# A scheduler that counts one-column matmuls by what they stream, with a new set of seeds

## The chip, the cores and the metric

The kernel runs on one core of one Trainium2 chip. The core has a matrix engine (TensorE, PE in the profile, with PEld for its weight loads), a vector engine (VectorE, DVE), a scalar engine (ScalarE, ACT) that evaluates functions such as exp, a general engine (GpSimd, POOL) and a queue that issues DMAs (SyncE, SP). Each engine works through its own queue in order and waits on semaphores where it needs another engine's result. The metric is the time of one execution on the device, in microseconds (us), as the median of the runs shown.

## What is computed

One transformer block with adaptive layer norm. The input x is 2048 rows of 512; there are 32 heads of 16 columns.

```python
mod = (silu(c) @ w_mod).reshape(1, 6, 1, 512)
sa, ca, ga, sb, cb, gb = (mod[:, i] for i in range(6))
h = layernorm(x) * (1 + ca) + sa
x = x + ga * mha(h, wqkv, wo)                  # 32 heads, softmax over 2048 keys
h = layernorm(x) * (1 + cb) + sb
x = x + gb * (gelu(h @ w1 + b1) @ w2 + b2)     # w1: 512 x 1376
```

All inputs are bfloat16. c is one row of 512, so each of the six modulation vectors is a product of one row with a 512 x 512 matrix. sa and ca are called the first modulation here (modA), sb and cb the second (modB).

## The kernel before

**Tiling.** Queries are worked in four blocks of 512 rows, keys in 16 tiles of 128. A run is one query block with four heads; there are 32 runs (in the last block each run has eight heads with half the queries). For each run and key tile PE makes four score blocks of 512 columns (L803), each with 128 keys as weights in 32 rows of the array (the columns of two heads, with the queries masked to one of them). A score block goes one of two ways:

- to ACT: the blocks are taken three and two at a time in turn (PSUM tiles st), and one instruction at L852 writes the exponentials (pt);
- to DVE: four blocks of a key tile go to PSUM tiles ax, and DVE turns them into the bit patterns of powers of two (L900, then shifted copies at L953 and L932 that are summed). POOL takes slices of 128 of the last shifted copy (L938) where it can work beside DVE.

The PV matmuls at L994 add all of these into one PSUM bank, od: per key tile four matmuls of 32 columns each, side by side in the array. At the end of a run DVE copies od out (L1019); the first PV matmul of the next run waits for that copy, since there is one od bank. The copy is divided by the row sums by way of DMAs and POOL (`normalise`, L1046), and the projection, second layer norm, Gelu (L1236) and MLP of each block are worked in between later runs (`block_tail`); those of the last half block come at the end (`last_half`).

**The order of the work.** It is not written by hand. A planner (`Plan`) runs while the program is built: it keeps, for each engine, the operations that are ready with a guessed duration, and repeatedly commits the one that can start first. Among operations that could start within a small slack of each other, `pick` takes the lowest of priority plus `spread`. `spread` is a pseudo-random number drawn from the operation's number and a seed; there is one seed for every 12.5 us of planned time (`SEEDS`), and a seed divisible by 4 gives no random part. So a seed changes the order of all that follows it.

**Zero matmuls.** `commit` keeps a list, `done`, of PE's operations of the last 30 us with the time that each is counted to have streamed. It walks back through the list until the sum reaches 1.45 us (`HEAT`); that operation's time plus 3.4 us (`WIN`) becomes `cool`. When the planner's time has passed `cool`, a PV operation gets a set of four zero matmuls with it (`extra`, L446 in `zeros`), and `step` may put in a matmul of zeros of its own (`heat`, L430, L435, or `zeros` at L446). Before the first scores `step` doesn't look at `cool` and fills every gap. `fill_at` is found in the same way with 1.6 us, and holds back work that isn't due.

**The modulations.** `mod_columns` makes eight columns for each modulation. A column is four matmuls whose moving operand is one column (L575), with 128 x 128 weights from w_mod. In the second modulation every other column is followed by a matmul of zeros with 384 columns (L578, `warmer`). The planner's duration for a column was 0.36 us in the second modulation and 0.22 us in the first, and these were also what `done` counted as streamed. A chain of such pieces is made by `chain`.

At the start the first modulation's weights (blk at L502) are loaded behind the first rows of x. DVE takes statistics of x (L599, L600), POOL makes 1/sqrt (L604, L606), DVE normalises (z, L610), PE transposes z (L652), and DVE and ACT apply the modulation (blk, L618 and L615). Then come keys and queries (L693), values (L732), the copy of the keys (kT, L623 on ACT), the masked queries (qm, L711), and the first scores.

Of the kernel before, what the change touches and what calls it, by code (L numbers as in the profile page):

```python
# [53 lines left out]
AL = 0.31  # L54
FILL = 1.6
SPREAD = 0.3
SEEDS = (0, 754, 829, 213, 501, 185, 582, 565, 437, 42, 790, 462, 0, 754, 457, 839, 409, 0, 203, 962, 735, 761, 634, 310, 991, 550, 943, 962, 775, 874, 0, 773, 813, 994, 107, 0, 718, 755, 523, 613, 695, 751, 275, 363, 273, 389, 697, 823, 85, 41, 155, 101, 0, 0, 0, 559, 994, 0, 0, 0, 0, 0, 0, 0, 0, 0)
HEAT = 1.45


class Res:


    def __init__(self, name, n, alloc):
        self.name, self.alloc = name, alloc
        self.free = [0.0] * n


class Op:
    count = 0  # L70

    def __init__(self, eng, fn, us, deps=(), lat=0.14, prio=5.0, mode=None, kind="", acq=None,
                 rel=(), gate=None, port=False):
        self.port = port
        self.eng, self.fn, self.us, self.lat, self.prio = eng, fn, us, lat, prio
        self.mode, self.kind, self.acq, self.rel, self.gate = mode, kind, acq, rel, gate
        self.end = None
        self.ready = 0.0
        self.tile = None
        self.slot = None  # L80
        self.kb, self.due, self.extra = 0, 1e9, False
        self.uses = 0
        self.rows, self.cont, self.run = None, False, None
        self.waiters = []
        self.todo = 0
        self.seq = Op.count
        Op.count += 1
        for d in deps:
            if d is None:
                continue  # L90
            if d.end is None:
                d.waiters.append(self)
                self.todo += 1
            else:
                self.ready = max(self.ready, d.end)
        for owner in rel:
            owner.uses += 1


class Plan:  # L100
# [51 lines left out]
    def spread(self, o):  # L152
        seed = SEEDS[min(int(self.now // 12.5), len(SEEDS) - 1)]
        x = (o.seq * 2654435761 ^ seed * 2246822519) & 0xFFFFFFFF
# [25 lines left out]
    def commit(self, s, o):  # L180
        self.lists[o.eng].remove(o)
        self.now = s
        if o.acq is not None:
            o.slot = min(range(len(o.acq.free)), key=lambda i: o.acq.free[i])
            o.acq.free[o.slot] = 1e18
            o.tile = o.acq.alloc(o.slot)
        if o.kind == "pv" and s >= self.cool and o.last_left() > 1:
            o.extra, o.us = True, 2 * o.us
        if o.rows is not None:
            o.row = min(o.rows, key=lambda i: self.tiles.get(i, 0.0) if self.mode == "qk" else i)  # L190
            o.mode = ("qk", o.row)
        if o.eng == "PE":
            self.done.append((s, (o.us if o.mode[0] != "qk" else o.us * (len(o.mode) - 1) / 4)))
            while self.done[0][0] < s - 30.0:
                self.done.popleft()
            tot = 0.0
            self.fill_at = self.cool = 0.0
            for t, us in reversed(self.done):
                tot += us
                if tot >= HEAT and not self.cool:  # L200
                    self.cool = t + WIN
                if tot >= self.fill:
                    self.fill_at = t + WIN
                    break
            if o.mode[0] != self.mode:
                self.mode, self.tiles = o.mode[0], {}
            for i in o.mode[1:]:
                self.tiles[i] = s + o.us
            self.free["PE"] = s + 0.01
        else:  # L210
            self.free[o.eng] = s + o.us
            if o.port:
                self.port[o.eng] = s + o.us
            if o.eng == "DVE" and o.us > 0:
                self.dve = (s, s + o.us, o.port)
        o.end = s + o.us + o.lat
        if o.kb:
            q = "SP"
            self.bus[q] = max(self.bus[q], s + o.us + 0.9) + o.kb / (300.0 if s < 12.0 else 260.0)
            o.end = self.bus[q] + 0.7  # L220
        if o.fn is not None:
            o.fn(o)
        for owner in o.rel:
            owner.uses -= 1
            owner.last = max(getattr(owner, "last", 0.0), o.end + (DVE_PE if o.eng == "DVE" else 0.0))
            if owner.uses == 0:
                owner.acq.free[owner.slot] = owner.last
        for w in o.waiters:
            w.todo -= 1
            w.ready = max(w.ready, o.end + (DVE_PE if o.eng == "DVE" and w.eng == "PE" else 0.0))  # L230
            if w.todo == 0:
                self.lists[w.eng].append(w)
# [21 lines left out]
def kernel(  # L254
# [57 lines left out]
    ps = scores.enter_context(tc.tile_pool(name="ps", bufs=1, space=psum))  # L312
# [81 lines left out]
    def chain(pieces, deps, kind, acq, rel=(), steps=1, need=None):  # L394

        first = prev = None
        at, step = due_now
        for n, (fn, us) in enumerate(pieces):
            last = n == len(pieces) - 1

            def go(o, fn=fn):
                if first is not None and o is not first:
                    o.tile, o.acq, o.slot = first.tile, first.acq, first.slot
                fn(o.tile)
            o = Op("PE", go, us, (tuple(deps) if prev is None else (prev,)) + (() if need is None else (need(n),)), lat=PEL if last else 0.0, mode=("full", 0),
                   kind=kind, acq=acq if prev is None else None, rel=rel if last else ())
            o.due = at + step * (steps * n // len(pieces))
            o.cont = prev is not None
            plan.add(o)
            first = first or o  # L410
            prev = o
        due_now[0] += steps * step
        return prev
# [165 lines left out]
                             rhs=warm[:, 0:1].to_broadcast([P, QB - P]))  # L579

    def mod_columns(dst, ws, kind, warmer=True):
        mm = chain([(lambda ps, n=n, w=w, m=m: mod_mm(ps, n, w[1](), m, warmer), 0.36 if warmer else 0.22)
                    for n, w in enumerate(ws) for m in range(NC)],
                   [o_sc, o_warm, ws[0][0]], kind, r_ax, [w[2] for w in ws],
                   need=lambda i: ws[i // NC][0])

        def out_(o):
            nc.vector.tensor_copy(out=dst, in_=mm.tile[:, 0:2 * NC])
            nc.vector.tensor_scalar(out=dst[:, NC:2 * NC], in0=dst[:, NC:2 * NC], scalar1=1.0,
                                    scalar2=None, op0=ALU.add)  # L590
        return op("DVE", out_, 0.4, (mm,), prio=0.65, rel=(mm,))
# [895 lines left out]
```

## Time and profile before

| | us |
|---|---|
| median of 3 runs (lowest, highest) | 780.99 (780.62, 781.88) |
| profiled execution, time | 779.58 |
| its span, first to last instruction | 777.8 |
| ACT busy | 750.5 |
| PE busy | 722.0 |
| DVE busy | 712.7 |
| POOL busy | 281.2 |

The profile is of one execution. Each line of a group gives the source line, the engine, the operation, what it writes and reads by the program's names, the count, then busy time and mean duration, then the idle time of the engine ahead of these instructions and what ended it. A line of a timeline gives the start, the duration and the instruction, and in brackets the idle time before it with its releaser. A line of the busy time by stretches gives the stretch, its length, then the busy time of PE, PEld, DVE, ACT and POOL with the number of instructions in brackets, the granted TensorE clock as a share of full speed, the DMA engines' share and GB/s. A line of the chain gives the start, the duration and the work that the end depended on.

### The profile page before, as it was taken

The page shows a single profiled execution, that of the slowest core. Times are in us where ns is not written, and L with a number is a line of the kernel's source. Part 1 is how long each engine was busy: PE and PEld are TensorE (multiplying, and loading weights), DVE is VectorE, ACT ScalarE, POOL GpSimd, SP SyncE. Part 2 cuts the span into 40 slices and gives each one's busy share as a digit, 9 for nine tenths or more (in the row PEclk, how much of TensorE's full clock was granted, in tenths as well). Part 3 has the DMA queues.
Part 4 walks back from the last instruction along what each step waited for, and adds up shares of the span by engine and source line. Part 5 has one row for each costly group of instructions (what it writes and reads, how often), then busy time and mean ns, then how long its engine had stood idle before and what let it go on. Part 6 is the DMA issues. An engine that isn't in the chain of part 4 may idle for free.

```text
span 777.8 us, 20624 instructions
## 1 busy us (share of the span) xinstructions
PE 722.0 (93%) x8233; PEld 274.2 (35%) x8307; DVE 712.7 (92%) x1180; ACT 750.5 (96%) x680; POOL 281.2 (36%) x622
## 2 busy tenths in 40 slices
PE   8888999999999889999998999999999999989998
PEld 3433333233333232323332323223234444434455
DVE  6777999999899999999999989999989998999964
ACT  3999999999999999999999999999999999999994
POOL 5221433444533334454444433333322423233320
PEclk9999998999999999999999999999999999999999
DMA  7033011000011010000100010000111000100010
GB/s 217 28 107 124 16 27 43 12 24 13 22 43 54 23 47 23 19 6 22 44 20 21 15 35 16 26 23 16 39 48 29 22 22 16 46 25 18 25 46 28
DMA packets 39074, 28.23 MB, mean 36 GB/s; under 512 B 17957, under 2 KB 34374, under 8 KB 38978
## 3 DMA queue, kind: packets, MB, share of 16 engines
q1 hardware_dynamic: 38970, 26.91, 12.1%
q8 instruction: 65, 1.06, 0.6%
q14 instruction: 31, 0.25, 0.1%
q10 hardware_dynamic: 8, 0.00, 0.0%
HBM read 21.30 MB, written 2.61 MB: 31 GB/s over the span
## 4 chain that ended last, share of the span: by engine, by line
ACT 50%; PE 27%; DVE 12%; issue 9%; DMA 1%; POOL 0%; SPq 0%; ACTq 0%; DVEq 0%; POOLq 0%
ACT pt L852 46%; PE od L994 9%; PE st L803 8%; DVE ph L900 5%; PE ax L1157 3%; DVE sh L953 2%; ACT g L1236 2%; PE ax L803 2%; DVE ph L953 1%; PE ax L693 1%; DMA blk<-in_w_mod_dram 1%; DVE sl L932 1%; DVE g L1227 1%; PE ax L1217 1%; PE t L1157 1%
## 5 line engine op out<-in xcount | busy, mean ns | idle before, releaser
L852 ACT ACTIVATE pt<-st 128x1536 bf16<-128x1536 f32 x626 | 708.6, 1408 | 4.4 <-PE st L803 2.3
L900 DVE TENSOR_SCALAR ph<-ax 128x512 int16<-128x512 f32 x484 | 318.1, 682 | 25.2 <-PE ax L803 22.3
L938 POOL TENSOR_TENSOR sl<-ph,step 128x128 int32<-128x128 int32 x358 | 163.7, 459 | 327.3 <-DVE sh L953 105.3
L803 PE MATMUL st<-qm,kT 32*128 32x512 bf16 x1564 | 245.7, 384 | 32.5 <-ACT pt L852 25.0
L803 PEld LDWEIGHTS <-kT 32*128 32x128 bf16 x2048 | 86.6, 91 | 244.1 <-issue 232.5
L803 PE MATMUL ax<-qm,kT 32*128 32x512 bf16 x484 | 162.5, 381 | 3.5 <-DVE ph L900 2.8
L994 PEld LDWEIGHTS <-VEB 128*32 128x32 bf16 x4992 | 109.6, 96 | 150.2 <-issue 128.0
L994 PE MATMUL od<-pt,VEB 128*32 128x512 bf16 (+1 forms) x1952 | 150.8, 344 | 0.9 <-ACT pt L852 0.5
L953 DVE TENSOR_SCALAR sh<-ph 128x4096 int16<-128x4096 int16 x121 | 146.9, 1217 | 2.5 <-PE od L994 2.2
L994 PE MATMUL od<-ph,VEB 128*32 128x512 bf16 (+1 forms) x1216 | 90.1, 340 | 1.7 <-DVE OD L1019 1.0
L994 PE MATMUL od<-sh,VEB 128*32 128x512 bf16 (+1 forms) x1216 | 84.6, 340 | 1.6 <-DVE sh L953 0.8
L953 DVE TENSOR_SCALAR ph<-ph 128x2048 int16<-128x2048 int16 x121 | 83.0, 687 | 0.4
L932 DVE TENSOR_SCALAR sl<-ph 128x1024 int16<-128x1024 int16 (+3 forms) x121 | 57.7, 482 | 0.4 <-PE od L994 0.4
L1046 POOL TENSOR_TENSOR OT<-OD,RB 128x128 bf16<-128x128 f32 x76 | 35.4, 470 | 48.1 <-DVE sh L953 14.8
L994 PE MATMUL od<-sl,VEB 128*32 128x512 bf16 (+1 forms) x608 | 48.4, 342 | 0.3
L1217 PE MATMUL ax<-blk,W 128*128 128x512 bf16 (+1 forms) x142 | 39.2, 358 | 2.0 <-issue 0.8
L1046 POOL TENSOR_TENSOR OS<-OD,RB 128x128 bf16<-128x128 f32 x48 | 22.8, 476 | 39.4 <-DVE sl L932 15.6
L693 PE MATMUL ax<-blk,w 128*128 128x512 bf16 x100 | 33.4, 383 | 3.3 <-ACT blk L615 1.7
L1227 DVE TENSOR_SCALAR g<-ax,b1c 128x512 bf16<-128x512 f32 (+1 forms) x41 | 28.0, 691 | 3.9 <-PE ax L1217 3.0
L1157 PE MATMUL ax<-w,g 128*128 128x512 bf16 x101 | 28.9, 381 | 1.1 <-DVE ph L900 0.6
L599 DVE BATCH_NORM_STATS2 ln_s<-xb 128x6 f32<-128x512 bf16 x32 | 21.6, 676 | 1.4 <-DMA xb<-in_A_x_dram 1.3
L1157 PEld LDWEIGHTS <-g 128*128 128x128 bf16 x176 | 13.7, 97 | 22.5 <-issue 12.8
(112 smaller groups left out, 400.8 us busy)
## 6 DMA issues: line engine op xcount, KB each, us to landing
RB<-rn SPq DMA_DIRECT2D x124, 64.0 KB
xb<-in_A_x_dram SPq DMA_DIRECT2D x8, 512.0 KB
out_dram<-o SPq DMA_DIRECT2D x16, 128.0 KB
qm<-qs SPq DMA_DIRECT2D x120, 16.0 KB
W<-in_B_w_dram SPq DMA_DIRECT2D x1, 1376.0 KB
w<-in_A_wqkv_dram SPq DMA_DIRECT2D x3, 384.0 KB
blk<-in_w_mod_dram SPq DMA_DIRECT2D x2, 512.0 KB
g<-in_w_mod_dram SPq DMA_DIRECT2D x2, 512.0 KB
```

Source lines behind the costliest of these rows:

```text
L693: return chain([(lambda ps, j=j: nc.tensor.matmul(out=ps[:, 0:QB], lhsT=w.tile[:, j, cc * P:(cc + 1) * P], rhs=o_h[b].tile[:, j, :], start ...
L803: nc.tensor.matmul(out=o.tile[:, k * QB:(k + 1) * QB], lhsT=kT[cc][kb][rows, ko * P:(ko + 1) * P], rhs=qm.tile[rows, par, :] if hb is None ...
L852: nc.scalar.activation(out=e.tile[:, 0:len(got) * QB], in_=o.tile[:, 0:len(got) * QB], func=ACT.Exp, scale=ESC)
L900: nc.vector.tensor_scalar(out=ph.tile[:, c0:c0 + QB], in0=o.tile, scalar1=PH_B, scalar2=0.0, op0=ALU.add, op1=ALU.max)
L932: parts = [in_turn(op("DVE", lambda o: nc.vector.tensor_scalar(out=into.tile[:, 0:cols], in0=first.tile[:, 0:cols], scalar1=PH_SH[-1], sca ...
L938: after_dve(nc.gpsimd.tensor_tensor(out=into.tile[:, c].bitcast(I32), in0=first.tile[:, c].bitcast(I32), in1=step, op=ALU.add))
L953: o = op("DVE", lambda o: nc.vector.tensor_scalar(out=dst(o), in0=src(), scalar1=PH_SH[j], scalar2=None, op0=ALU.add), us, deps, lat=DL, p ...
L994: nc.tensor.matmul(out=o_od[r].tile[32 * i:32 * i + 32, n * HB:n * HB + w], lhsT=v_tile(kt)[:, c0:c0 + 32], rhs=got[i][:, at:at + w], star ...
L1046: two = beside(lambda c: nc.gpsimd.tensor_tensor(out=OT.tile[:, c], in0=OD.tile[:, c], in1=o5.tile[:, c], op=ALU.mult), (OT,), (OD, o5))
L1157: nc.tensor.matmul(out=ps, lhsT=g[:, f, col:col + P], rhs=rhs, start=(f == 0), stop=(f == NF - 1))
L1217: mm = chain([(lambda ps, f=f, j=j: nc.tensor.matmul(out=ps[:, 0:N], lhsT=W1[:, j, f * P:(f + 1) * P], rhs=h.tile[:, j, 0:N], start=(j == ...
L1227: ev.append(op("DVE", lambda o, f=f, mm=mm: nc.vector.tensor_scalar(out=g.tile[:, f, 0:N], in0=mm.tile[:, 0:N], scalar1=b1c[:, f:f + 1], s ...
```

## The change

A third element is allowed in a piece of a chain: the time that the planner counts as streamed. Only `mod_columns` gives it, 0.18 us for a column with odd number and 0.01 for one with even number, in both modulations, though the first has no matmul of zeros behind its columns. The planned durations stay. Of the 66 seeds, eight near the end are zero in both kernels and all others differ; none of the first 49 is zero now, where five of them were before. Lines below 409 of the source move down by one.

```diff
-SEEDS = (0, 754, 829, 213, 501, 185, 582, 565, 437, 42, 790, 462, 0, 754, 457, 839, 409, 0, 203, 962, 735, 761, 634, 310, 991, 550, 943, 962, 775, 874, 0, 773, 813, 994, 107, 0, 718, 755, 523, 613, 695, 751, 275, 363, 273, 389, 697, 823, 85, 41, 155, 101, 0, 0, 0, 559, 994, 0, 0, 0, 0, 0, 0, 0, 0, 0)
+SEEDS = (589, 42, 869, 201, 842, 714, 286, 774, 871, 883, 670, 306, 195, 922, 117, 659, 193, 45, 151, 549, 170, 271, 319, 470, 749, 145, 287, 829, 529, 198, 510, 578, 819, 255, 730, 695, 454, 90, 99, 606, 462, 783, 435, 482, 134, 154, 446, 417, 301, 0, 693, 890, 0, 263, 0, 207, 778, 430, 526, 0, 731, 0, 0, 0, 0, 0)
...
-        self.kb, self.due, self.extra = 0, 1e9, False
+        self.kb, self.due, self.extra, self.act = 0, 1e9, False, None
...
-            self.done.append((s, (o.us if o.mode[0] != "qk" else o.us * (len(o.mode) - 1) / 4)))
+            self.done.append((s, o.act if o.act is not None else (o.us if o.mode[0] != "qk" else o.us * (len(o.mode) - 1) / 4)))
...
-        for n, (fn, us) in enumerate(pieces):
+        for n, (fn, us, *act) in enumerate(pieces):
...
             o.cont = prev is not None
+            o.act = act[0] if act else None
             plan.add(o)
...
-        mm = chain([(lambda ps, n=n, w=w, m=m: mod_mm(ps, n, w[1](), m, warmer), 0.36 if warmer else 0.22)
+        mm = chain([(lambda ps, n=n, w=w, m=m: mod_mm(ps, n, w[1](), m, warmer), 0.36 if warmer else 0.22, 0.17 * (m % 2) + 0.01)
                     for n, w in enumerate(ws) for m in range(NC)],
```

## The prediction

> **What bounds the kernel now.** First the busy shares and the costliest groups on the page.
>
> ```profile
> PE 722.0 (93%) x8233; PEld 274.2 (35%) x8307; DVE 712.7 (92%) x1180; ACT 750.5 (96%) x680; POOL 281.2 (36%) x622
> ...
> L852 ACT ACTIVATE pt<-st 128x1536 bf16<-128x1536 f32 x626 | 708.6, 1408 | 4.4 <-PE st L803 2.3
> ```
>
> ScalarE (ACT) is busy for 96% of the span, and 708.6 of its 750.5 us are the exponentials of L852: 1564 score blocks of 512 columns at 708.6/1564 = 0.453 us each. Between the first exponential (15.79) and the last (754) ACT does little but these, so the time is the start, plus ACT's work, plus ACT's gaps, plus the tail. The same group with its shapes kept apart:
>
> ```profile
> L852 ACT ACTIVATE pt<-st 128x1536 bf16<-128x1536 f32 x313 | 507.6, 1622 | 2.9 <-PE st L803 2.0 <-PE ax L803 0.9
> L852 ACT ACTIVATE pt<-st 128x1024 bf16<-128x1024 f32 x312 | 373.0, 1196 | 1.5 <-PE ax L803 1.0 <-PE st L803 0.3
> ```
>
> The records overlap: a pair lasts 1.622 + 1.196 = 2.82 us, yet five blocks advance by 5 x 0.453 = 2.27. So each record hides some 0.28 us, and a gap that is shown costs 0.28 more than its idle time. From start to start, the trace has 1.331 and 0.904 us where ACT is dense; what exceeds this I call a stall.
>
> Then busy time by stretches of 2 us around the largest gap, and ACT's own timeline there:
>
> ```profile
> 130.00:132.00 2.00, 1.73 (x24) 0.95 (x24) 2.00 (x4) 2.00 (x4) 0.30 (x1) 1.00 0.14 36
> 132.00:134.00 2.00, 1.68 (x15) 0.40 (x14) 2.00 (x3) 2.00 (x3) 0.46 (x1) 0.51 0.30 99
> 134.00:136.00 2.00, 2.00 (x19) 0.60 (x15) 1.09 (x6) 1.55 (x3) 0.43 (x1) 0.50 0.01 4
> 136.00:138.00 2.00, 2.00 (x20) 0.57 (x19) 1.43 (x6) 2.00 (x3) 1.27 (x3) 0.50 0.00 0
> 138.00:140.00 2.00, 2.00 (x27) 0.43 (x19) 1.66 (x4) 1.13 (x2) 0.46 (x1) 0.79 0.04 8
> ```
>
> ```profile
> 134.98 3.28 ACT L852 ACTIVATE pt<-st 128x1024 bf16<-128x1024 f32 x3 [0.45 <-PE ax L803]
> 139.13 11.40 ACT L852 ACTIVATE pt<-st 128x1536 bf16<-128x1536 f32 x10 [0.87 <-PE ax L803]
> ```
>
> The column ahead of the DMA share is the granted TensorE clock. It is halved for about 6.8 us from 132.0, and only here between start and tail. The 32 one-column matmuls of the second modulation (L575) run from 128.5 to 135.6: the clock falls in the middle of them. In the halved stretch PE is full and ACT waits twice.
>
> Third, the start, because the order changes there:
>
> ```profile
> 8.32 0.99 DVE L610 TENSOR_SCALAR z<-xb,mv,rs 128x512 bf16<-128x512 bf16 x2 [0.61 <-POOL rs L606]
> ...
> 10.37 0.71 DVE L589 TENSOR_SCALAR modA<-modA 128x4 f32<-128x4 f32 x1
> ...
> 11.19 0.99 DVE L618 TENSOR_SCALAR blk<-st,modA 128x512 bf16<-128x512 bf16 x2
> ...
> 11.77 1.45 ACT L615 ACTIVATE blk<-st,modA 128x512 bf16<-128x512 bf16 x2 [3.86 <-DVE blk L618]
> ...
> 15.79 6.88 ACT L852 ACTIVATE pt<-st 128x1536 bf16<-128x1536 f32 x6 [1.52 <-PE st L803]
> ...
> 25.12 0.59 ACT L623 CAST kT<-ax 128x512 bf16<-128x512 f32 x1 [1.11 <-PE ax L693]
> ...
> 26.20 3.71 ACT L852 ACTIVATE pt<-st 128x1536 bf16<-128x1536 f32 x3 [0.48 <-PE st L803]
> ```
>
> The normalised rows z are ready at 9.3, before the modulation's weights have landed (9.57), so they cost nothing. ACT later waits 1.11 and 0.48 us for the second block's keys.
>
> Last, the chain at one of the 31 changes from one run of heads to the next:
>
> ```profile
> 617.41 0.61 DVE OD L1019
> 618.02 0.04 issue
> 618.07 0.40 PE od L985 x4
> 618.47 0.87 PE od L994 x32
> 619.34 0.34 PE st L803 x2
> ```
>
> The single od bank must be copied out (L1019) before PE can go on, and od matmuls stand ahead of the next scores; ACT ran dry at 619.7 for 0.44 us, start to start.
>
> **The change, part by part.** *Work.* Counted by line and shape in the two orders of instructions, ACT, SP and all arithmetic of PE are the same in number. PE has 11 more full-width zero matmuls (26 to 32 at L430, 10 to 15 at L435) and one set of four fewer at L446 (104 to 100). POOL takes 15 more slices (358 to 373), and DVE's sl instructions shrink by 15 x 256 columns; by the sl forms (480, 546 and 611 ns for 1280, 1536 and 1792 columns) that is 15 x 0.066 = 1.0 us. DVE is idle 8% and ACT never waits on POOL, so I take 0; the ends are -1.0 and +0.5.
>
> *The second modulation.* Before, 24 one-column matmuls stand between score blocks 238 and 248, with one set of four PV matmuls among them. After, the 32 are spread over blocks 295 to 315, at most eight between two groups of scores, with two to five sets of PV matmuls in most gaps and one set of zeros at block 310. Streams of 512 columns follow each other 0.22 us apart (sixteen od matmuls in fours take 1.05, four alone 0.39). Over eight blocks (3.6 us) the leanest stretch streams 1.1 us before and 1.45 after. I take the dip as gone. It is worth 0.45 + 0.87 + 2 x 0.28 = 1.88 us. Ends: 0 (dip back) and -1.9.
>
> *The start.* Two things are put in order differently. DVE now has the modA copy and scale ahead of the four z; before they were behind. And PE has nine zero matmuls behind the modulation and ahead of the transposes. Step by step: modulation on PE ends at 10.1 as before (its DMAs are issued first, as before). modA is done by 10.6 (0.18, modB's price for the same scale) to 11.1 (0.71, its own row). The four z take 1.5 to 1.8 (rows 0.83 + 0.99, or 0.70 + 0.73 for the next block), to 12.1 to 12.9. The zeros end at 10.1 + 9 x 0.22 = 12.1, within that. Transposes then need 0.6 more, so DVE's blk starts about 13.2 to 13.5, not 11.19: +2.0 to +2.3. The q matmuls of the first three slices are now queued ahead of the last k matmul, which gains about 0.4. The first exponential comes at 17.4 to 17.7: +1.6 to +1.9. Behind it DVE's remaining three statistics, the V copy and z of block two end at 22.0 to 22.4 (21.7 before), because one statistic has moved ahead of qm. ACT then runs 5 exponentials (5.8), two blk (1.45), one exponential and kT with no 1.11 wait, and reaches the exponential that started at 26.20 at 26.6 to 26.95. Of the delay +0.4 to +0.75 is left; a gap of 0.54 at 44.0 may take some of it. I take +0.5; ends 0 and +1.9 (if nothing is absorbed).
>
> *Run changes.* I call a change uncovered where at most three score blocks, and at most 0.45 us of matmuls, stand between the last od matmul of a run and the first of the next. Before has 7 such; their stalls sum to 1.29 us (0 to 0.44, mean 0.185). The rest sum to 1.03, mean 0.045. After has 12. At the same means: 12 x 0.185 + 18 x 0.045 = 3.0 against 2.3, so +0.7. Ends: all at 0 (-1.5) and all at 0.44 (+3.8).
>
> *The tail* has the same operations in nearly the same order from the last exponential on: 0, ends -0.3 and +0.5.
>
> Sum: -1.9 + 0.5 + 0.7 = -0.7 us. The profiled execution took 779.58 (span 777.8), hence 778.9; the median 780.99 is 1.4 above it, and I carry the difference over: 780.3.
>
> **The rivals.**
> Faster: the start is absorbed in full (the 0.54 gap takes the rest) and the run changes cost what they do now. Then the dip's 1.9 stays whole: 779.1. For it speaks that ACT has slack before 44 us; against it the count of 12.
> The change doesn't do what it says: the clock falls again, in a lean stretch elsewhere, such as the 4.9 us Gelu of L1236 during which ACT takes no scores, so PE can idle. Before has this too without a dip. Then +0.5 + 0.7 = +1.2: 782.2.
> The dip is not in every run: the lean stretch lasts little longer than half of the 6.8 us for which the clock stays down, so a small shift in time may decide. If half of the timed runs are free of it now, the gain in the median is 0.94 and the sum +0.3: 781.2. Against it speaks that the profiled execution has the dip and is the fastest of the four known times, and that the other three lie within 1.3 us, less than the dip's price. [...]
> Slower: PE's wait for the od copy at uncovered run changes. All at 0.44 gives -1.9 + 0.5 + 3.8 = +2.4: 783.4. It turns the sign past the bound when the mean of the twelve exceeds 0.37. For it speaks that the od work behind the copy is 0.65 us or more at eight of the twelve; against it that two of the seven cost nothing.
>
> **How the numbers follow.** About 0.2%, 1.56 us, is what a measurement tells from no change, so the bounds are 779.4 and 782.6. Chances: the forecast 0.28, the faster rival 0.26, the dip's return 0.16, the dip in some runs only 0.08, the slower rival 0.22. Faster by over 0.2%: most of the faster rival and a little of the forecast, 0.29. Slower: nearly all of the slower rival, a third of the dip's return and a little of the forecast, 0.28. Within: 0.43. The range reaches to both outer rivals and a little under the faster one for fully covered run changes: 778.2 to 783.4.
>
> **What would show it.** Right: granted clock 1.00 through the modulation (57 score blocks, some 26 us, later than now) and no ACT gap there; first exponential near 17.5 with no wait of about 1.1 before the second kT; ACT gaps after L1019. Wrong: a halved clock elsewhere, the seventh exponential later than 26.95, more than 0.37 us lost at each uncovered run change, or a longer tail.

## The result and the profile after

The changed kernel takes 781.90 us in the median of 22 runs (780.81 to 784.81); the kernel before, on the same chip, 780.69 us (22 runs, 778.09 to 782.92). The ratio is 1.002, with a 95% interval of 1.0011 to 1.003: slower by 1.2 us in the medians, where 0.7 us less was forecast. The profiled execution took 781.21 us with a span of 779.4 us, against 779.58 and 777.8 before.

From the page of the changed kernel, busy time and the costliest group:

```profile
PE 729.7 (94%) x8314; PEld 275.9 (35%) x8314; DVE 712.1 (91%) x1180; ACT 751.1 (96%) x680; POOL 291.1 (37%) x637
...
L853 ACT ACTIVATE pt<-st 128x1536 bf16<-128x1536 f32 x626 | 709.2, 1401 | 3.2 <-PE st L804 1.7
```

ACT's work is the same (709.2 against 708.6 us for the exponentials), so what was gained and lost lies in the start, the gaps and the tail, as the prediction had it. ScalarE's timeline at the start:

```profile
13.72 1.45 ACT L616 ACTIVATE blk<-st,modA 128x512 bf16<-128x512 bf16 x2 [5.26 <-DVE blk L619]
16.26 0.59 ACT L624 CAST kT<-ax 128x512 bf16<-128x512 f32 x1 [1.09 <-PE ax L694]
17.34 5.97 ACT L853 ACTIVATE pt<-st 128x1536 bf16<-128x1536 f32 x5 [0.49 <-PE st L804]
...
25.75 0.59 ACT L624 CAST kT<-ax 128x512 bf16<-128x512 f32 x1 [0.20 <-PE ax L694]
26.82 3.71 ACT L853 ACTIVATE pt<-st 128x1536 bf16<-128x1536 f32 x3 [0.49 <-PE st L804]
```

The first exponential comes at 17.34 (15.79 before), the seventh at 26.82 (26.20): of the first delay of 1.55 us, 0.62 is left. Busy time by stretches of 2 us where the second modulation (L576, 155.0 to 164.5) now runs:

```profile
156.00:158.00 2.00, 1.78 (x25) 0.69 (x23) 2.00 (x4) 2.00 (x3) 0.00 (x0) 1.00 0.04 9
158.00:160.00 2.00, 1.77 (x27) 0.87 (x26) 1.72 (x3) 2.00 (x3) 0.87 (x2) 1.00 0.00 0
160.00:162.00 2.00, 1.74 (x28) 0.80 (x24) 1.06 (x2) 2.00 (x3) 1.21 (x3) 1.00 0.00 0
```

The granted clock is 1.00 here, as it is from 6.9 to 778.3: the dip is gone. The chain at one of the uncovered run changes:

```profile
458.73 0.70 DVE OD L1020
459.43 0.04 issue
459.48 0.83 PE od L995 x12
460.31 0.32 PE st L804 x2
460.63 0.00 PE ax L804
460.63 0.36 PE od L995 x4
460.99 0.02 issue
461.01 0.56 ACT pt L853
```

The copy of od, then od matmuls ahead of the scores: ACT loses 0.49 us here, start to start. Two engines' work can meet at such a place too; this is the chain ahead of the largest stall near a run change, 0.78 us:

```profile
209.69 0.70 DVE VEB L626
210.39 0.04 issue
210.43 0.39 PE od L995
210.82 0.32 PE ax L694
211.15 0.32 PE st L804 x3
```

The scores stand behind a matmul for keys (L694), and that behind an od matmul that waits for the copy of the values (L626). Both kernels run the same 626 exponentials, so their starts can be laid side by side, after minus before:

| exponential (its start before) | difference, us |
|---|---|
| 1st (15.8) | +1.55 |
| 26th (50.7) | +0.63 |
| 126th (165.1) | -0.52 |
| 176th (221.6) | +0.62 |
| 401st (483.4) | +1.11 |
| 526th (633.3) | +0.08 |
| 626th (754.1) | +0.89 |
| end of the span | +1.64 |

In sums: the dip takes away 1.86 us; the start leaves 0.62; the stalls of the exponentials around the 31 copies of od grow from 2.32 to 5.08 us (+2.75); all other stalls shrink by 0.45; and from the end of the last exponential to the end of the span it is 23.73 instead of 22.98 us (+0.75).

### The profile page after: what moved, and what is told of

Read it like the earlier page. It is cut to its first block, busy times and chain, and to the rows that moved or that the text cites. A ratio compares the mean times of both kernels' runs of the same rounds, so it can differ in the third digit from the quotient of the medians.

```text
span 779.4 us, 20714 instructions
## 1 busy us (share of the span) xinstructions
PE 729.7 (94%) x8314; PEld 275.9 (35%) x8314; DVE 712.1 (91%) x1180; ACT 751.1 (96%) x680; POOL 291.1 (37%) x637
## 4 chain that ended last, share of the span: by engine, by line
ACT 53%; PE 26%; DVE 11%; issue 9%; POOL 1%; POOLq 0%; ACTq 0%; DVEq 0%
ACT pt L853 51%; PE od L995 10%; PE st L804 7%; DVE ph L901 4%; DVE sh L954 2%; PE ax L1158 2%; PE ax L804 1%; PE ax L1218 1%; DVE ph L954 1%; DVE OD L1020 1%; PE ax L431 1%; PE ax L694 1%; PE t L1158 1%; DVE sl L933 1%; DVE z L611 0%
## 5 line engine op out<-in xcount | busy, mean ns | idle before, releaser
L853 ACT ACTIVATE pt<-st 128x1536 bf16<-128x1536 f32 x626 | 709.2, 1401 | 3.2 <-PE st L804 1.7
L939 POOL TENSOR_TENSOR sl<-ph,step 128x128 int32<-128x128 int32 x373 | 172.0, 462 | 318.9 <-DVE sh L954 111.3
L804 PE MATMUL ax<-qm,kT 32*128 32x512 bf16 x484 | 159.0, 380 | 3.4 <-DVE ph L901 3.2
L995 PE MATMUL od<-pt,VEB 128*32 128x512 bf16 (+1 forms) x1952 | 148.0, 341 | 1.8 <-DVE OD L1020 0.9
L995 PE MATMUL od<-sh,VEB 128*32 128x512 bf16 (+1 forms) x1216 | 86.3, 339 | 2.0 <-DVE sh L954 1.2
L1218 PE MATMUL ax<-blk,W 128*128 128x512 bf16 (+1 forms) x164 | 42.0, 361 | 0.0
L694 PE MATMUL ax<-blk,w 128*128 128x512 bf16 x124 | 36.7, 382 | 2.1 <-ACT blk L616 2.0
L1158 PE MATMUL ax<-w,g 128*128 128x512 bf16 x112 | 31.0, 382 | 0.6 <-DVE ph L901 0.4
L1020 DVE COPY OD<-od 128x512 f32<-128x512 f32 x31 | 21.2, 683 | 1.3 <-PE od L995 1.2
```

Of the source, the lines that this page charges most:

```text
L694: return chain([(lambda ps, j=j: nc.tensor.matmul(out=ps[:, 0:QB], lhsT=w.tile[:, j, cc * P:(cc + 1) * P], rhs=o_h[b].tile[:, j, :], start ...
L804: nc.tensor.matmul(out=o.tile[:, k * QB:(k + 1) * QB], lhsT=kT[cc][kb][rows, ko * P:(ko + 1) * P], rhs=qm.tile[rows, par, :] if hb is None ...
L853: nc.scalar.activation(out=e.tile[:, 0:len(got) * QB], in_=o.tile[:, 0:len(got) * QB], func=ACT.Exp, scale=ESC)
L939: after_dve(nc.gpsimd.tensor_tensor(out=into.tile[:, c].bitcast(I32), in0=first.tile[:, c].bitcast(I32), in1=step, op=ALU.add))
L995: nc.tensor.matmul(out=o_od[r].tile[32 * i:32 * i + 32, n * HB:n * HB + w], lhsT=v_tile(kt)[:, c0:c0 + 32], rhs=got[i][:, at:at + w], star ...
L1020: OD = op("DVE", lambda o: nc.vector.tensor_copy(out=o.tile, in_=od.tile), 0.6, (last,), prio=0.0, acq=r_OD, rel=(od,))
```

## The experiments

In all comparisons it helps to look at the mean granted clock of each timed run, which tells how many microseconds of it TensorE spent at half clock (0.995 in the profile of before, with 6.83 us of it between start and tail). A run at 0.999 or 1.000 is called undisturbed below: its clock falls only in the last microseconds (from 778.3 us in the profile of the changed kernel, at 0.999).

### The count and the seeds, one at a time

The changed kernel with the old seeds (e1), and the kernel before with the new seeds (e2):

```diff
-SEEDS = (589, 42, 869, ...
+SEEDS = (0, 754, 829, ...
```

> The new count with the old seeds. Theory (the order that the seeds drew costs the time; the count pays): the clock stays at full speed through the second modulation, worth 1.9 us; the count shifts the order behind it as well, which I give +-1.5. So 778.8, between 777.3 and 780.3. Rival (the dip costs the median nothing, and any new order costs about 1 us): 781 to 782.5, whether the clock dips or not.

> The new seeds with the old count. Theory: the nine zero matmuls and the late z of the start remain (+0.6), the one-column matmuls stand closer again and the clock dips (+1.9 against the changed kernel): 783 to 784. Rival (the count does nothing): as the changed kernel, 781.9 within 0.8.

Measured: 804.01 us (ratio 1.0295, 1.0273 to 1.0317) and 802.32 us (1.0279, 1.026 to 1.0298). Every expectation missed by some 20 us. The exponentials' group on the page of the first, then of the second:

```profile
L853 ACT ACTIVATE pt<-st 128x1536 bf16<-128x1536 f32 (+1 forms) x634 | 719.5, 1389 | 16.4 <-PE st L804 7.6
```

```profile
L852 ACT ACTIVATE pt<-st 128x1536 bf16<-128x1536 f32 (+1 forms) x632 | 717.3, 1387 | 16.5 <-PE st L803 10.0
```

There are more exponentials (634 and 632, not 626) and 16 us of idle time ahead of them where 3 to 4 were; start to start, between exponentials with no other work of ACT in between, the stalls sum to 23.4 and 24.1 us (9.2 and 9.6 in the two kernels of the case). In e2, 7.28 us of idle time is a single wait, at 536.5, for scores behind 22 matmuls of L1217. Both had halved clock too: e1 at 132.2 to 142.5, 422.4 to 429.2 and 473.6 to 477.0, even with the new count, and e2 at 319.5 to 322.9 and 439.0 to 445.8. So neither half has an effect of its own that could be added to the other's. Both runs pair a count with seeds that weren't chosen for it, and both cost over 20 us. The change is a step from one chosen order to another, and only the two orders can be compared.

### Zeros in the second modulation of the kernel before

```diff
-        if m % 2 and warmer:
+        if warmer:
```

> The kernel before, with a matmul of zeros of 384 columns behind all eight columns of the second modulation instead of four; the order of everything else is that of before. Theory: the granted clock stays at 1.00 from 128 to 140 us, ACT's gaps of 0.45 and 0.87 us go, and the last exponential ends at 753.0 instead of 754.84; 1.9 us less than before in the same run, 778.8. Rival (the dip is hidden or not in most runs): clock at 1.00 but less than 0.7 us gained.

Measured: 780.13 us (778.34 to 781.89, 12 runs), ratio 0.999 (0.9974 to 1.0005). The 778.8 of the theory was missed in the median. In its profile the dip at 132 is gone, and with it three stalls that sum to 1.86 us in before; some 0.3 of this comes back soon, since by the 126th exponential the kernel is 1.49 us ahead of the first profile of before, and from 193 to 576 us it stays 1.52 to 1.54 ahead. Then it loses it again in two places: at 603 to 608 (1.47 us, see the last section) and at a new dip of 3.41 us at 686.2, beside the Gelu (1.16 us). Three of the twelve runs are undisturbed, and these take 778.34 to 779.05.

### The kernel before, profiled a second time

> The kernel before itself, profiled a second time. Theory (TensorE's clock is decided once per window of 3.41 us, by the work that fell into that window, and the windows start at a chance moment): the clock is halved for one or more whole multiples of 3.41 us, near 127-139 us in any case, and perhaps at 682-690 as well; away from the halved stretches the exponentials start at the same distances as in the first profile, within 0.3 us in sum. Rival (the dip belongs to the order alone): one dip at 132.0 for 6.8 us again, and nothing else.

Measured: 781.01 us in the median of 8 runs; the profiled one has a span of 779.2 us. Busy time in stretches of 3.41 us, then those around the Gelu:

```profile
126.71:130.12 3.41, 2.88 (x36) 1.28 (x32) 3.41 (x7) 3.41 (x5) 1.77 (x4) 1.00 0.03 2
130.12:133.54 3.42, 3.33 (x31) 0.94 (x27) 3.36 (x5) 3.42 (x4) 0.45 (x1) 0.50 0.24 77
133.54:136.95 3.41, 3.41 (x34) 1.06 (x34) 2.27 (x8) 2.97 (x4) 1.70 (x4) 0.50 0.01 2
136.95:140.36 3.41, 3.41 (x31) 0.63 (x23) 2.13 (x4) 2.19 (x2) 0.45 (x1) 0.50 0.02 5
140.36:143.78 3.42, 3.42 (x46) 0.99 (x45) 2.84 (x5) 3.04 (x3) 1.37 (x3) 1.00 0.00 0
683.08:686.50 3.42, 1.87 (x37) 1.14 (x41) 3.42 (x6) 3.39 (x3) 1.53 (x4) 1.00 0.03 7
686.50:689.91 3.41, 3.19 (x32) 1.11 (x28) 2.11 (x5) 3.39 (x2) 0.46 (x1) 0.50 0.05 10
```

The clock is halved for 10.24 us from 130.1 and for 3.41 from 686.5. Against the first profile this costs 0.88 us more in the first place and 1.19 in the second; everywhere else behind the start the exponentials stand at the same distances to within 0.05 us. So the stalls belong to the order and come in both profiles; the dips differ, 6.83 us in the first against 13.65. That settles what the median of before is made of. Over the 104 timed runs of before whose clock is known:

| mean granted clock | runs | median, us |
|---|---|---|
| 0.999 | 5 | 778.04 |
| 0.995 | 25 | 778.82 |
| 0.993 | 37 | 780.67 |
| 0.991 | 12 | 781.61 |
| 0.990 and below | 21 | 782.5 |

The other four (0.996) lie between 780.69 and 781.73; why these are slower than those at 0.995 isn't known. 3.41 us at half clock lower the mean by 0.0022 (half of 3.41 in 777.8). The profile on which the prediction rests was one at 0.995, with a smaller dip than most.

### The changed kernel, profiled a second time

> The changed kernel itself, timed in the same call as the three kernels that are compared with it. If its stalls belong to its order of work, a second profile shows them at the same places: ScalarE's exponentials lose 9.9 us from start to start, within 0.5, around the run changes 5.1, and the granted clock stays at 1.00 from the start's end to the last microseconds. If they are chance, the list of stalls changes by more than 1 us. Time against before: ratio 1.002, some 781 to 783.

Measured: 781.58 us (781.18 to 783.64, 12 runs), ratio 1.0015 (1.0002 to 1.0028). The stalls are the same to 0.03 us at every place but two: 0.18 at 606, and 1.03 at 50 to 51, where this run had a dip of 3.41 us (47.3 to 50.8). With the first 22 runs, 20 of 34 are undisturbed, at a median of 781.48 us. The half that the profile could not show is this: without any dip, the new order is 3.4 us slower than the old one (781.48 against 778.04). What it saves is dips: they take 0.3 us of its median, where before loses 2.7. It isn't free of them, as the other 14 runs have a mean clock of 0.998 or less.

### The start

On DVE the copy and scale of modA go behind the four z, and the nine zero matmuls are left out:

```diff
+        hush[0] = not warmer and n == 1 and m == NC - 1
...
+            if kind == "modA":
+                late_mod.append(lambda: put(o))
+            else:
+                put(o)
...
+        n_z[0] += 1
+        if n_z[0] == TPB:
+            late_mod.pop()()
```

> The changed kernel with before's order at the start: the copy and scale of modA stand behind the four z on DVE, and the nine zero matmuls behind the first modulation are left out. Theory: the first exponential comes back from 17.3 to 15.8-16.0, the seventh from 26.8 to 26.2-26.3, and the 0.6 us that was left there reaches the end: 0.4 to 0.8 us less than the changed kernel in the same call. Rival 1: ACT catches the 0.6 up later, in waits that are tied to other engines: 0, within 0.2. Rival 2: the whole delay of the first exponential counts: 1.5 less.

Measured: 780.76 us (779.72 to 781.99, 12 runs), 0.8 less than the changed kernel beside it; its four undisturbed runs take 779.72 to 779.90. On ScalarE:

```profile
16.72 5.97 ACT L874 ACTIVATE pt<-st 128x1536 bf16<-128x1536 f32 x5 [0.49 <-PE st L825]
...
26.20 3.71 ACT L874 ACTIVATE pt<-st 128x1536 bf16<-128x1536 f32 x3 [0.48 <-PE st L825]
```

The seventh exponential is back at 26.20, 0.62 us earlier, and through 600 exponentials to the last one this stays between 0.62 and 0.67. The first is only 0.62 earlier, where 1.3 to 1.5 were expected, but at 25 us the second block's keys end the difference: the seventh is where before has it. So the term for the start was right for this pair, and nothing behind 27 us absorbs it. One pair fixes its size only roughly: with the changed kernel's start the seventh exponential comes at 26.53 to 26.99 in other profiles (after_again above, e4 and e8 below), with before's at 25.63 and 26.18 (before_again, e3). But the span is shorter by 1.48 us, and a second step, 0.82, falls between the last exponential and the end, where this kernel has the same orders as the changed one. This is taken up next.

### The tail

Two kernels. In e4 the last load of x brings only the two row tiles that are used (256 of 512 KB):

```diff
-            nc.sync.dma_start(out=o.tile, in_=x_src[b])
+            nc.sync.dma_start(out=o.tile[:, lo:TPB, :], in_=x_src[b][:, lo:TPB, :])
```

> The changed kernel, with the last load of x cut to the two row tiles that the last half block uses (256 KB instead of 512); nothing else moves. Theory: the first addition of the tail (L1302) starts at 759.4 because that load lands then; with half of it, it starts at 758.5 to 758.8 as its matmul ends, and the tail is 0.6 to 0.9 us shorter: 781.2. Rival (the addition waits for its own matmul or for DVE): no difference beyond 0.2 us in the trace.

Measured: 780.56 us (ratio 1.0009, 0.9996 to 1.0022), 780.50 undisturbed, so some 1.0 less than the changed kernel. In its profile the tail is shorter by 0.3 only. In e10 two sets of zero matmuls are left out:

```diff
-        for i in range(4):
+        n_zero[0] += 1
+        for i in range(0 if n_zero[0] in (24, 25) else 4):
```

> The changed kernel with two sets of four zero matmuls left out, at 640 and 703 us, where PE has much else to do: PE's list of instructions is 16 entries shorter from there on, and nothing else is changed. Theory: the tail is longer by 0.7 us because a fetch of 16 KB of PE's instructions gets onto the DMA engines 1.3 us behind the last exponential, and packets of the last load of x queue behind it; with 16 entries fewer the fetch comes some 0.5 us or more later, the load is through, the first addition of L1302 starts 2.9 us behind the last exponential and not 3.7, and the time falls by 0.6 to 0.9 us. Rival: the load is late for another reason, such as its four forerunners on SP's queue, and the tail stays 23.7 us.

Measured: 781.14 us (780.13 to 782.05), four undisturbed runs at 780.13 to 780.50, so 1.3 less than the changed kernel, where the tail in the two profiles differs by 0.8; the other 0.5 stays open. From the changed kernel, busy time in stretches of 0.5 us, 1.0 us and more behind the last exponential (its end is 755.71); the last two columns are the DMA engines' share and GB/s:

```profile
756.71:757.21 0.50, 0.50 (x4) 0.21 (x3) 0.47 (x2) 0.49 (x2) 0.00 (x0) 1.00 1.13 389
757.21:757.71 0.50, 0.50 (x5) 0.20 (x2) 0.47 (x2) 0.50 (x2) 0.00 (x0) 1.00 0.13 41
757.71:758.21 0.50, 0.50 (x4) 0.24 (x3) 0.09 (x1) 0.50 (x2) 0.00 (x0) 1.00 0.05 6
758.21:758.71 0.50, 0.50 (x6) 0.35 (x5) 0.00 (x0) 0.50 (x1) 0.00 (x0) 1.00 0.07 10
758.71:759.21 0.50, 0.50 (x7) 0.46 (x5) 0.00 (x0) 0.50 (x1) 0.00 (x0) 1.00 0.01 4
```

The same places of e10, whose last exponential ends at 756.54:

```profile
757.54:758.04 0.50, 0.45 (x3) 0.22 (x3) 0.47 (x2) 0.49 (x2) 0.00 (x0) 1.00 1.00 338
758.04:758.54 0.50, 0.50 (x4) 0.19 (x2) 0.47 (x2) 0.50 (x2) 0.00 (x0) 1.00 0.13 45
758.54:759.04 0.50, 0.50 (x4) 0.23 (x3) 0.10 (x1) 0.50 (x2) 0.00 (x0) 1.00 0.00 0
759.04:759.54 0.50, 0.50 (x6) 0.34 (x5) 0.09 (x1) 0.50 (x1) 0.00 (x0) 1.00 0.00 0
```

In the changed kernel the load's burst is over at 757.5, yet a trickle goes on for 1.3 us more; in e10 there is none. The packets of the trace tell what it is, in us behind the last exponential's end (queue 8 carries instructions, queue 1 the load):

```
changed kernel   queue 8   16384 B   1.31 to 2.23
                 queue 1    1024 B   2.21 to 2.34
                 queue 1    1024 B   2.32 to 2.45
                 ...        eight more, the last to 3.12
e10              queue 1    1024 B   the last to 1.83
                 queue 8   16384 B   1.48 to 2.42
```

A fetch of 16 KB of PE's instructions gets in front of the last ten packets of the load. That they share one DMA engine is inferred: the load ends with 16 writes of 4 bytes, and in the changed kernel 15 of them are through by 1.80 us, the last at 3.12. In e10 the fetch comes 0.17 us later, not 0.5 as expected, and that is enough. DVE's first addition of the tail, in the changed kernel and in e10:

```profile
759.42 0.69 DVE L1302 TENSOR_TENSOR xb<-t,xb 128x512 bf16<-128x512 f32 x1 [1.62 <-ACT g L1232]
```

```profile
759.45 0.69 DVE L1305 TENSOR_TENSOR xb<-t,xb 128x512 bf16<-128x512 f32 x1 [0.81 <-PE t L1301]
```

That is 3.71 and 2.91 us behind the last exponential. In e10 the matmul ends the wait; in the changed kernel the profile names an ACT instruction that had long been done, so the releaser is taken to be the load, whose last packet landed 0.59 us before. In e6, e8 and e11 (see below) the load is named as the releaser, and there the addition starts 0.56 to 0.59 us behind its last packet too. e10's tail is 22.91 us, and so is e5's, which has 18 instructions fewer; before has 22.98. The theory holds: the 0.75 us were not in the tail's own work, but in when a fetch of PE's instructions happens to come (1.31 us behind the last exponential, 1.48 in e10). e4 fits in part: there the fetch also came at 1.31 and still held back one packet, to 2.38; but the addition starts 1.03 us behind that, not 0.59, and why isn't known. Of the 1.0 us in e4's timed runs the tail explains 0.3; the rest stays open.

### The od copy at the run changes

First the copy itself was cut to half of its columns, with GpSimd filling the other half (e8):

```diff
-        OD = op("DVE", lambda o: nc.vector.tensor_copy(out=o.tile, in_=od.tile), 0.6, (last,),
+            nc.vector.tensor_copy(out=o.tile[:, 0:HB], in_=od.tile[:, 0:HB])
+            nc.gpsimd.memset(o.tile[:, HB:QB], 1.0)
```

> The changed kernel with half of each od copy of L1020: columns 0 to 255 are copied and GpSimd sets the others to 1, so half of the queries of every run but the last are left out of the result; the order of PE, ACT, SP and DVE is the same. It shortens the one wait that the theory blames, from 0.69 us to some 0.4, by about 0.3. Theory (PE stands at the od copy with scores queued behind it): the stalls of 0.49, 0.48, 0.36, 0.25 and so on around the run changes shrink by up to 0.3 each, their sum from 5.1 to 2.3-3.2, and the time falls by 1.5 to 2.7 us. Rival: the copy is not what comes last, the stalls are set by the amount of od and other matmuls ahead of the scores: the sum stays above 4.3 and the time falls by less than 0.7.

Measured: 781.98 us (780.68 to 784.27, 12 runs), ratio 1.0022 (1.0007 to 1.0036). In the profile eight stalls at copies shrink by 0.13 to 0.26 us each, 1.6 in sum, and the stalls around run changes go from 5.08 to 3.16, as the theory had it. But a new stall of 0.40 appears at 645.5, the last exponential ends only 0.7 us earlier, and the timed runs gain nothing. The same cut without GpSimd's part (e11):

```diff
+        OD = op("DVE", lambda o: nc.vector.tensor_copy(out=o.tile[:, 0:HB], in_=od.tile[:, 0:HB]), 0.6, (last,),
...
+                              in_=OD.tile[16:P:32, 0:HB].unsqueeze(1).to_broadcast([4, 2, HB]))
...
+            out=OT.tile[:, c], in0=OD.tile[:, slice(c.start % HB, c.start % HB + P)], in1=o5.tile[:, c],
```

> The changed kernel with half of each od copy of L1020 again, without any work on GpSimd in its place: the denominators' move and the products of L1048 read columns 0 to 255 twice, so half of the queries of every run but the last come out from the wrong sums; every engine has as many instructions as in the changed kernel, in the same order. Theory (the copy's length is what the exponentials wait for at the run changes, and the sets to 1 on GpSimd ate the gain in the timed runs of the other half copy): the eight stalls that shrank there shrink again, by 1.3 to 1.7 us in sum, nothing new of more than 0.2 us appears, and the undisturbed runs, 781.4 for the changed kernel, come to 779.5 to 780.3. Rival (what the copy gives, other engines take back): the eight stalls shrink, but the last exponential ends less than 0.9 us earlier, from its start, and the undisturbed runs stay above 780.7.

Measured: 780.82 us (780.31 to 782.25, 11 runs), undisturbed 780.62 (eight runs). One copy, in the changed kernel and in e11:

```profile
458.73 0.69 DVE L1020 COPY OD<-od 128x512 f32<-128x512 f32 x1
```

```profile
459.26 0.42 DVE L1020 COPY OD<-od 128x256 f32<-128x256 f32 x1
```

The copy is shorter by 0.27 us, and nine stalls shrink by 0.16 to 0.27 us, 2.2 us in sum: PE does stand at the copy with scores queued behind it. The exponentials gain only 1.04 of this from the first to the last: a new stall of 0.35 shows at 605, and the rest goes in steps of under 0.1. So the rival is nearer, though both of its bounds (0.9 us, 780.7) were passed by a little, where the theory's 780.3 was not reached. The timed runs don't show the copy alone: in e11's profile the tail is 24.65 us, 0.9 longer than in the changed kernel, by a fetch again (see the last section). PE is busy for 94% of the span and DVE for 91%; that ACT, where it no longer waits for the copy, runs up against them somewhat later would explain why about half of the saved waits comes back, but no run shows it. In e8 more than that is lost in the timed runs; GpSimd's sets to 1 are the only other difference, and why they cost so much was not followed up.

Then the order on PE was changed, with the copy as it was: the od matmuls of a new run wait in the emitter until the next group of scores is out.

```diff
+            if first or plan.held:
+                plan.held.append((work, owners))
+            else:
+                work()
+            if end:
+                plan.flush()
```

> The changed kernel with one thing moved on PE alone: the od matmuls of a new run that come before the next group of scores are issued behind that group; the copy is as long as it was, and nothing is left out. Theory: the scores no longer wait for the copy, so the stalls at the uncovered run changes (2.9 us) mostly go, and the time falls by 1.5 to 2.5 us. Rival: the held matmuls pile up behind the scores (up to eight sets, 1.8 us) and the group of scores after that comes late instead: stalls of the same sum, one exponential later, and a change of time within 0.5 us.

Measured: 796.44 us (792.42 to 800.55, 6 runs), ratio 1.0208 (1.0178 to 1.0239). This failed, and by more than the rival had it. The chain at the largest stall:

```profile
104.06 0.39 PE st L821 x3
104.45 1.27 PE od L1015 x16
105.73 0.54 PE ax L821
106.26 1.82 PE od L1015 x12
108.09 0.50 PE st L821 x2
...
108.69 2.37 ACT pt L870 x2
```

The group of scores is out in time, but 28 held od matmuls stand ahead of the next one, and the clock falls there as well (105.0 to 108.4): little else had gone through PE while they were held (4.5 by the measure of the last section). ACT waits 2.8 us. In this way the cost of a run change isn't saved, it comes back one group of scores later.

### The kernel before with its two lean stretches filled

```diff
-        if m % 2 and warmer:
+        if warmer:
...
-        for i in range(4):
+        n_zero[0] += 1
+        for i in range({12: 0, 24: 3}.get(n_zero[0] - 1, 1) * 4):
+            i %= 4
```

> The kernel before, with zero matmuls put into its two leanest stretches and nothing else moved: 384 zero columns behind each of the eight columns of the second modulation that a group issues (not every second one), and the set of four zero matmuls at 682 us, ahead of the Gelu, three times over; the set at 283 us, in a rich stretch, is left out, so that the number of PE's instructions between there and 682 us is that of before. Theory: the halved clock was what separated before's median from its undisturbed runs (777.6-778.1): at most half of the runs still see a dip, the median comes to 778.0-779.2, 0.2 to 0.4% under before and 0.4% under the changed kernel, and the granted clock is above 0.995 in most runs. Rival: the zeros cost PE what the dips did, or the clock falls elsewhere: median 780-781.

Measured: 778.47 us (777.34 to 779.52, 12 runs), ratio 0.9977 (0.9965 to 0.9988). Six of twelve runs are undisturbed, with a median of 777.90; one of 29 runs of before beside it was. This is the fastest of all kernels here, 2.0 us under before in the medians and 3.3 under the changed kernel's 34 runs, with eight more zero matmuls in the whole program, of which the planner knows nothing. In its profile (span 777.7) the only dip between start and tail is one at 10.5 us, ahead of the first exponential. The theory holds, and it shows what the change gave: fewer dips. It paid for them with a worse order.

## Why the prediction was wrong

*The dip.* Right that it goes, and about right in size for the one profile: 1.88 worked out, 1.86 by the starts of the exponentials in that same profile, and 1.5 in e3, where the dip alone was taken away. In the median the dips were worth more, 2.4 us (2.7 less 0.3), since most runs of before are longer at half clock than the profiled one.

*The rival "The dip is not in every run"* had the right mechanism and was argued away wrongly. The half of 6.8 us that it argues with is the 3.41 us of the traces (last section). That the profiled execution has a dip and is the fastest of four was read as a sign that dips are constant. They vary, but all runs of before except 5 in 104 have some, and the profile had one of the smaller ones. *"I carry the difference over"* (1.4 us from profile to median) fails for the same reason: that difference was dips. After the change the median is only 0.7 above the profiled time. The rival by which the clock falls again elsewhere is true of single runs (47.3 in after_again), though it doesn't set the median.

*The start.* Right step by step in this profile: DVE's blk 13.2 to 13.5 (13.15 found), first exponential 17.4 to 17.7 (17.34), seventh 26.6 to 26.95 (26.82), +0.5 taken and 0.62 found; e5 showed that all of it reaches the end. "A gap of 0.54 at 44.0 may take some of it" didn't happen: the gap is still there, at 44.65.

*Run changes: the step that failed most.* "At the same means: 12 x 0.185 + 18 x 0.045 = 3.0 against 2.3, so +0.7." The sum takes 30 changes where the kernel has 31; the missing one adds 0.05. PE does wait for od's copy, as it says, but the means don't hold: the twelve cost 0.24 each (2.90), the covered ones 0.11 each (2.17 in 19), 5.08 us in all and +2.75. The count depends on where the line is drawn. Taken from the profiles, with 0.22 us for each 512 columns, and DVE's scores counted among the matmuls, the two bounds give 10 uncovered changes before, at a mean of 0.14 us, and 13 after, at 0.24. So it isn't mainly the count that rose, it is the price of a change of the same kind. Of the covered part 1.09 us lie at 211 to 214, where not od's copy but a copy for the values (L626) and the keys behind it hold PE, and 0.28 at 104, where od's copy waits 1.03 us behind a shift of 1217 ns on DVE. That is what a rule by the number of score blocks can't see: these two run changes are dear because something else is in DVE's or PE's queue at the same time. The slower rival, with a bound of 0.37 for the mean of the twelve, was not reached, and yet the sign turned, because the covered ones and the tail came on top.

*The tail.* "The same operations in nearly the same order: 0." The order was the same, and the tail was 0.75 longer, above the upper end of 0.5. The missing term was not in any engine's order.

*The sum.* For the profiled run: -1.86, +0.62, +2.75, -0.45 for other stalls and +0.75 make +1.81; less 0.17 in the small distances of the exponentials that gives the +1.64 of the spans. Undisturbed, the new order costs 3.4 us. e5, with the old start and with a tail as short as before's, takes 779.76, so 1.7 of the 3.4 are start and tail, and 1.7 lie between (2.1 by the two profiles). That the latter are the run changes is shown for the part that hangs on od's copy (e11); for the rest it is read from the stalls in the profiles, and no run took them away.

## What to carry to other kernels

Before comparing two kernels by one profile each, look at the granted clock of many timed runs: time without dips and time lost to dips are two numbers, and a change can move them in opposite directions. In a kernel whose order comes from a search, a change of the planner's counting couldn't be judged alone; if only the clock is to be kept up, put zeros into the leanest stretches and leave the order as it is, as e9 did with two (778.47 us in the median against 780.52). Where three engines are over 90% busy, don't count on all of a removed wait: of 2.2 us in e11 1.04 was left, of 1.86 in e3 1.5, and of the start's 0.62 in e5 all.

## What the runs showed of the hardware

**When the clock falls.** In all traces of this case every dip ahead of the tail has a length of 3.41, 6.83 or 10.24 us and begins a multiple of 3.41 us after the clock's first rise (126.29 us in both profiles of before, which is 37 times 3.413, half of the first profile's dip of 6.827 us). That rise comes at 5.73 us in the first of these profiles and at 3.83 (130.12 less 126.29) in the second. A stretch of 3.41 us between two such moments is called a window here. What went through PE ahead of a dip can be counted in the traces as well: take each matmul by its columns and by the share of the array's rows and columns that its weights fill, so that a matmul of 512 columns with 32 of 128 weight columns is a quarter, and one of one column next to nothing. A window could hold nearly 16 full ones of 512 columns, which start 0.217 us apart at the closest (L430 in before, L431 in the changed kernel). With the window taken to end 0.2 us before the fall, which separates best, all 14 dips begin behind a window with 2.0 to 6.0. Behind 20 us no window under 5.75 was spared, but for one of 5.5 in before, where 74 matmuls have no record; no dip began above 6.0, and from 5.75 to 6.0 both happen (20 windows were spared). The weights and the 0.2 us were chosen on these same 14 traces, so this is a fit and not a tested rule. PE's busy time does not tell: in the stretch from 126.71 above, ahead of three halved windows, PE is busy for 2.88 of 3.41 us. The leanest window at any place has 4.0 in before (at 129.4) and 4.3 (at 681.9), 5.5 in the changed kernel, and 5.5 and 6.2 at these two places in e9. If the fit holds, the kernel before dips in the modulation wherever its windows begin, or nearly so; this is an estimate from the 4.0 and the 5.75. Measured is that 99 of its 104 runs have a dip.

**Instruction fetches are DMA traffic.** The page lists them, here for the changed kernel:

```profile
q1 hardware_dynamic: 38970, 26.91, 12.1%
q8 instruction: 65, 1.06, 0.6%
```

These are 65 packets of 16 KB, where PE's list has 16628 entries (8314 matmuls and as many weight loads): one for 256 of them. From one packet to the next PE starts 256 entries in the mean, by the records 255.8 in the changed kernel and 254.1 in before, where 74 are missing. That these are PE's instructions is inferred from that. Each packet takes 0.9 to 1.5 us here, up to 2.3 in e11. In the changed kernel's tail the load behind such a fetch came late: its last packet landed at 3.12 us, where 15 of the 16 writes that end the load were through by 1.80, and the addition started 0.59 us behind it. The fetch cost 0.75 us in the changed kernel's tail, 1.7 in e11's profile (first addition 4.63 us behind the last exponential, 32 packets behind a fetch of 2.28 us), and it hit a small transfer in e3. DVE at a reciprocal, first in before, then in e3:

```profile
601.32 0.25 DVE L1030 RECIPROCAL dc<-dc 128x16 f32<-128x16 f32 x1
```

```profile
601.46 0.25 DVE L1030 RECIPROCAL dc<-dc 128x16 f32<-128x16 f32 x1 [1.57 <-DMA dc<-dn]
```

In e3 a fetch from 599.16 to 600.38 held the row of 64-byte packets that should have landed a microsecond earlier; DVE stood 1.57 us, and the exponentials lost 1.47. In before the same fetch came at 601.43, behind it. In e3 the fetch at 600 us is 2.27 us earlier than in before, where the exponentials are 1.53 ahead: the other 0.74 us is put down to the four zero matmuls that stand at 130 us in PE's list, which is an estimate. In e9, which has them too but leaves out four others at 283 us, the fetch comes at 600.97 and DVE doesn't wait.
